# Attention units of a fused attention and feed-forward kernel: another order of ScalarE's, VectorE's and GpSimd's steps

## The chip, the cores and the metric

One core of a Trainium2 chip runs the whole program. The metric is the device time of one execution in microseconds (us). A number with a plain "us" is from one profiled execution; the times of repeated runs are given as their median.

The engines are TensorE (PE; its weight loads PEld), VectorE (DVE), ScalarE (ACT), GpSimd (POOL) and SyncE (SP), which issues most DMAs. Every engine takes its instructions in the order of its own queue and waits, at each, for the semaphores of what that instruction needs.

## The reference, cut to what matters

```python
scores = q @ k.T / sqrt(D)                       # B=2, H=8, S=768, D=64
is_global = pos[None, :] < n_global              # n_global = 8
is_local = (rel >= 0) & (rel < n_local)          # rel = row - column, n_local = 96
dist = where(is_global & ~is_local, n_local, abs(rel))
scores = where(is_global | is_local, scores - slope[h] * dist, -1e9)
a = exp(scores - max); a = a / (a.sum() + 1e-9)
x = (a @ v), heads side by side                  # 1536 tokens x 512
h = x @ w_in;  x = (h * sigmoid(h)) @ w_out      # 512 -> 2048 -> 512
h = x @ w_in2; y = (h * clip(h + 3, 0, 6) / 6) @ w_out2
```

The weights are 64-bit floats in memory; the kernel decodes them on the chip into a high and a low half.

## The kernel before, in words

**Attention units.** The attention is cut into 16 units: a batch, a half of the 768 rows (384 rows, three tiles t of 128) and a pair of heads. Only the keys near a tile and the first 32 are used, so a tile's scores are 128 wide (first tile of a first half) or 256 wide. Unit u takes three steps, n = 3u, 3u+1 and 3u+2, called a, b and c here; the loop over n runs from 0 and calls `attention_loop(n)`, then at most one feed-forward piece, then `turns(n)`, then the weight steps that fall due.

- Step a: `scores` (line 362; TensorE, 12 products into four PSUM banks of the tags S and o), `values(u-2)` (line 411: TensorE's products of the transposed exponentials with the values, `psO`; ScalarE's copy of the high half, line 424; VectorE's low half `xl`, line 425, is put in front of step b), the exponentials of t = 0, the division of the unit before (`normalise`), and `stage_a(u+1, 0)`: three or four transposes of the keys, ScalarE's copy of them (line 350) and VectorE's one or two small copies into the same tile (lines 351, 353).
- Step b: `xl`, the exponentials of t = 1, and `stage_a(u+1, 1)`: transposes of the queries and ScalarE's scaling of them (line 331), without which the next unit's scores can't start; then the loads of unit u+3.
- Step c: the exponentials of t = 2, and `turn(u-1)` (line 396): transposes of the three tiles of exponentials of the unit before, tile by tile, and their copies to SBUF (t = 0 and 2 on VectorE, line 408; t = 1 on ScalarE, line 406).

`exponentials(u, t)` is, for each of two heads, a VectorE pass that adds the bias to the scores and takes the extreme (line 379), then ScalarE's exponential with the sum beside it (line 383). `normalise` is two tiny VectorE steps on the sums (lines 388, 389) and six scalings on GpSimd (line 393). `patterns` (line 274) makes the two distance tiles from the two input words, `biases(p)` (line 309) scales them on GpSimd for a pair of heads, `beyond` (line 297) sets a flag that is read much later.

**PSUM.** The tag `tr` has three banks; into them go, in this order in every unit, the value products, the transposed keys, the transposed queries, and the three tiles of transposed exponentials. The tag `f` has one bank, for feed-forward pieces beside the attention and for the warm-up products.

**Beside the attention.** From n = 17 on, a piece of the first feed-forward layer goes into TensorE's queue at every second step at most (h pieces of 12 products at n = 17, 23, 29, 35, 41, 47; y pieces of 6 at 31, 33, 37, 39, 43, 45, 49, 51). A weight block of 512 columns is decoded in ten steps, started at n = 0, 6, 12, 18, 26, 32, 38 and 44. Counted from the start s, at the end of the step: `upper` s (ScalarE), `lower` s+1 (ScalarE), clamp s+1 (VectorE, line 986), shift s+2 (line 992), sign s+3 (line 998, two inputs), power s+4 (line 1003), scale s+5 and add s+6 (GpSimd, two inputs, lines 126 and 134), high half s+8 (ScalarE, line 145), low half s+9 (GpSimd, line 148). The piece of n = 17 needs the blocks of s = 0 and 6. From n = 54 on only feed-forward work is left.

**What sets the order.** In a `manual_schedule` region the named engines issue in the order of the program text; an engine that is not named is ordered by the scheduler, which may move a step ahead of or behind others. For the attention steps the region names TensorE, ScalarE and GpSimd (line 770), not VectorE. The prelude (line 734) is a region of all engines.

Of the kernel before, what the change touches and what calls it, by code (L numbers as in the profile page):

```python
# [18 lines left out]
P = 128  # L19
# [9 lines left out]
def attention_ffn_kernel(ctx, tc, q, k, v, n_global, n_local, w_in1, w_out1, w_in2, w_out2, out):  # L29
    nc = tc.nc  # L30
# [3 lines left out]
    NP = H // 2  # L34
    NT = S // P
    HB = 3
# [25 lines left out]
    def bank(tag, name):  # L62
        return psum.tile([P, 512], F32, name=name, tag=tag, bufs=ps_bufs[tag])
# [11 lines left out]
    def load_weights():  # L75
        n = loaded[0]
        if n == len(pieces):
            return
        loaded[0] += 1
        i, j = pieces[n]  # L80
        l, c = chunks[i]
        w_in, w_out = (w_in1, w_out1) if l == 0 else (w_in2, w_out2)
        fw = FC * P
        r = wpool.tile([P, DW, 2], I32, name=f"raw{n}", tag="raw", bufs=2)
        if j < 2:
            src = w_in.bitcast(I32)[2 * j * P:2 * (j + 1) * P, 2 * c * fw:2 * (c + 1) * fw].rearrange("(k p) f -> p k f", p=P)
            nc.sync.dma_start(r.rearrange("p (k f) w -> p k (f w)", k=2), src)
        else:
            row = c * fw + (j - 2) * P
            nc.sync.dma_start(r.rearrange("p e w -> p (e w)"), w_out.bitcast(I32)[row:row + P, :])  # L90
        raws[n] = r
# [122 lines left out]
    units = [(b, half, p) for b in range(B) for half in range(2) for p in range(NP)]  # L214
# [45 lines left out]
    t1 = apool.tile([P, HB, 2, W], F32, name="pat1", tag="z", bufs=ZB)[:, 0]  # L260
# [48 lines left out]
    def biases(p):  # L309

        nbs[p] = [cpool.tile([P, 2, w], F32, name=f"{n}{p}", tag=f"{n}{p}") for n, w in (("nbB", P), ("nbA", W))]
        for nb, dist in zip(nbs[p], (distB, distA)):
            for h in range(2):
                nc.gpsimd.tensor_scalar(out=nb[:, h, :], in0=dist, scalar1=slopes[2 * p + h], scalar2=1.0, op0=ALU.mult, op1=ALU.mult)
# [40 lines left out]
    zt, mnt, smt, ptt, scored = {}, {}, {}, {}, {}  # L355

    def width(u, t):
        return P if units[u][1] == 0 and t == 0 else W

    def scores(u):  # L360

        kt, qt = tr[u]
        two, one = ([bank(tag, f"psS{u}_{tag}{h}") for h in range(2)] for tag in "So")
        place = {(h, t): one[h][:, :W] if t == 2 else two[h][:, t * W:(t + 1) * W] for h in range(2) for t in range(HB)}
        for t in range(HB):
            for h in range(2):
                hs = slice(h * D, (h + 1) * D)
                o = P if width(u, t) == P else t * SP
                nc.tensor.matmul(place[h, t], qt[hs, t * P:(t + 1) * P], kt[hs, o:o + W], start=True, stop=True)  # L369
        scored[u] = place  # L370
        zt[u] = apool.tile([P, HB, 2, W], F32, name=f"z{u}", tag="z", bufs=ZB)
        mnt[u] = apool.tile([P, HB, 2], F32, name=f"mn{u}", tag="mn")
        smt[u] = apool.tile([P, HB, 2], F32, name=f"sm{u}", tag="sm")

    def exponentials(u, t):
        p, w = units[u][2], width(u, t)
        nb, z, mn, sm = nbs[p][w == W], zt[u], mnt[u], smt[u]
        for h in range(2):
            nc.vector.tensor_tensor_reduce(  # L379
                out=z[:, t, h, :w], in0=scored[u][h, t][:, :w], in1=nb[:, h, :], scale=1.0, scalar=3e38,  # L380
                op0=ALU.add, op1=ALU.min, accum_out=mn[:, t, h:h + 1])
        for h in range(2):
            nc.scalar.activation(out=z[:, t, h, :w], in_=z[:, t, h, :w], func=AF.Exp, bias=mn[:, t, h:h + 1], scale=-1.0,  # L383
                                 accum_out=sm[:, t, h:h + 1])

    def normalise(u):
        z, sm = zt[u], smt[u].rearrange("p t h -> p (t h)")
        nc.vector.tensor_scalar(out=sm, in0=sm, scalar1=1e-9, scalar2=None, op0=ALU.add)
        nc.vector.reciprocal(sm, sm)  # L389
        for t in range(HB):  # L390
            w = width(u, t)
            for h in range(2):
                nc.gpsimd.tensor_scalar(out=z[:, t, h, :w], in0=z[:, t, h, :w], scalar1=smt[u][:, t, h:h + 1], scalar2=1.0,  # L393
                                        op0=ALU.mult, op1=ALU.mult)
# [16 lines left out]
    def values(u):  # L411
# [12 lines left out]
        nc.scalar.copy(hi, ps[:, :TB])  # L424
        return lambda: nc.vector.tensor_tensor(out=lo, in0=ps[:, :TB], in1=hi.bitcast(F32), op=ALU.subtract)

    NS = HB * len(units)
    queue, late, rests, now = {}, {}, {}, [0]

# [3 lines left out]
    def attention_loop(n):  # L433
        u, t = divmod(n, HB)
        for f in queue.pop(n, []):
            f()
        if t == 0 and u < len(units):
            scores(u)
        if t == 0 and 0 <= u - 2 < len(units):
            at(n + 1, values(u - 2))  # L440
            if u < len(units):
                loads_v(u)
        if u < len(units):
            exponentials(u, t)
            if t == HB - 1 and u + 1 < NP:
                biases(u + 1)
        if n == 0:
            beyond()
        if t == 0 and 0 <= u - 1 < len(units):
            normalise(u - 1)  # L450
        for f in rests.pop(n, []):
            f()
        if t < 2 and u + 1 < len(units):
            stage_a(u + 1, t)
            if t and u + 3 < len(units):
                loads(u + 3)
# [241 lines left out]
    for l, c in chunks:  # L698
        first_piece[l, c] = len(stream)
        if fast(l, c):  # L700
            p = [(product, l, c, i) for i in (1, 6, 5, 7, 2, 4, 3)]
# [4 lines left out]
            h, y = H(l, c, 2), Y(l, c, 0)  # L706
# [3 lines left out]
        if (l, c) == (1, 0):  # L710

            h = H(l, c, 0) + H(l, c, 1) + H(l, c, 2)
# [21 lines left out]
    with tc.manual_schedule(engines=None):  # L734
        nc.vector.memset(three, 3.0)
        warm = fpool.tile([P, 512], F32, name="warm", tag="a")
        nc.vector.memset(warm, 0.0)
        for _ in range(3):
            nc.tensor.matmul(bank("f", "psW"), warm[:, :P], warm, start=True, stop=True)  # L739
        for i, ap in enumerate((n_global, n_local)):  # L740
            nc.sync.dma_start(nwords[:, i, :], ap.bitcast(I32).partition_broadcast(P))
        loads(0)
        make_identity(nc, ident)
        positions()
        loads(1)
        load_weights()
        loads_v(0)
        load_weights()
        loads(2)
        loads_v(1)  # L750
        load_weights()
        stage_a(0, 0)
        stage_a(0, 1)
        patterns()
        biases(0)
    todo = {when(i): f for i, f in enumerate(stream)}

    def loop(n):
# [8 lines left out]

    E = mybir.EngineType
    end = NS + LAG + 2
    with tc.manual_schedule(engines={E.PE, E.Activation, E.Pool}):  # L770
        for n in range(end):
            if n == NS + LAG:
                ready[0] = 1
            loop(n)
# [261 lines left out]
```

## Time and profile before

| what | value |
|---|---|
| median of 3 runs | 636.79 us (635.80 to 637.16) |
| the profiled execution's own time | 634.86 us |
| its span | 632.8 us |
| TensorE, busy | 606.6 us, 96% of the span |
| VectorE, busy | 464.5 us, 73% |
| ScalarE, busy | 412.9 us, 65% |
| GpSimd, busy | 160.4 us, 25% |
| mean granted clock of TensorE | 0.992 |

The span runs from the first to the last instruction of the profiled execution; some 2 us of the execution's time lie outside it. In the rows below a record has its start, its length, the engine, the line of the kernel, what it writes and reads, and in brackets how long its engine had been idle before it and what ended the wait. A granted clock (PEclk) of 1.00 is the upper of TensorE's two levels, 0.50 the lower. [...]

### The profile page before, as it was taken

To read this page: it belongs to the slowest core of one execution; us is meant where nothing else is said; L and a number is where in the kernel's file an instruction comes from. 1 tells how busy PE (TensorE), PEld (TensorE's weight loads), DVE (VectorE), ACT (ScalarE), POOL (GpSimd) and SP (SyncE) were. 2 spreads that over 40 slices of the span, in tenths; PEclk is the share of its full clock that TensorE was granted. 3 is DMA by queue.
4 is the path that set the end of the run, shared out by engine and by line. 5 is a ranking of instruction groups with operands and counts; after the bars stand their busy time and mean duration, and the time that the engine had idled before them with its cause. 6 is when DMAs were issued, how large, how long until landed. Compare 5 with 4: busy or idle time off the path is not lost.

```text
span 632.8 us, 9365 instructions
## 1 busy us (share of the span) xinstructions
PE 606.6 (96%) x3124; PEld 496.4 (78%) x3124; DVE 464.5 (73%) x1012; ACT 412.9 (65%) x863; POOL 160.4 (25%) x233
## 2 busy tenths in 40 slices
PE   6877999999999999999999999999999999999996
PEld 3656778898888788888888877887788888888885
DVE  5776777734588786767674779987979696969453
ACT  4785878755566676666666676765766666666760
POOL 2764867770111111111111110011111111111100
PEclk9998999999999999999999999999999999999998
DMA  7665556367767858686867791196577768776544
GB/s 173 154 157 124 128 142 147 87 195 141 157 129 158 186 135 183 151 186 151 186 152 154 161 207 67 67 266 151 136 174 163 176 162 177 160 183 151 100 109 162
DMA packets 81622, 97.29 MB, mean 154 GB/s; under 512 B 55456, under 2 KB 55456, under 8 KB 81312
## 3 DMA queue, kind: packets, MB, share of 16 engines
q0 software_dynamic: 12576, 45.09, 38.1%
q1 hardware_dynamic: 68992, 51.53, 27.2%
q8 instruction: 27, 0.44, 0.3%
q14 instruction: 27, 0.22, 0.1%
HBM read 46.27 MB, written 3.15 MB: 78 GB/s over the span
## 4 chain that ended last, share of the span: by engine, by line
PE 58%; issue 23%; POOL 6%; DVE 5%; ACT 5%; DMA 2%; POOLq 0%; DVEq 0%; SPq 0%; ACTq 0%
PE psY L655 25%; PE psH L482 15%; POOL y L684 4%; PE psP_b L563 3%; PE psO L421 3%; PE psT L403 2%; PE psP_c L563 2%; PE psP_a L563 2%; PE psS_S L369 2%; ACT z L383 2%; DMA y<-st 1%; POOL z L393 1%; PE psW L739 1%; PE psS_o L369 1%; DVE z L379 1%
## 5 line engine op out<-in xcount | busy, mean ns | idle before, releaser
L684 POOL DMA_DIRECT2D y<-st x78 | 66.9, 857 | 364.3 <-ACT st L680 359.1
L680 ACT COPY st<-psY 128x512 f32<-128x512 f32 x156 | 91.5, 587 | 52.0 <-PE psY L655 47.9
L482 PE MATMUL psH<-xh,wih 128*128 128x512 f32 (+1 forms) x216 | 83.3, 386 | 2.1 <-DVE g L513 1.5
L482 PE MATMUL psH<-xh,wil 128*128 128x512 f32 (+1 forms) x216 | 82.7, 383 | 2.3 <-POOL wil L148 2.3
L482 PE MATMUL psH<-xl,wih 128*128 128x512 f32 (+1 forms) x216 | 82.7, 383 | 0.0
L655 PE MATMUL psY<-gh,woh 128*128 128x512 f32 (+1 forms) x160 | 61.4, 384 | 0.0
L655 PE MATMUL psY<-gh,wol 128*128 128x512 f32 (+1 forms) x160 | 60.6, 379 | 0.0
L655 PE MATMUL psY<-gl,woh 128*128 128x512 f32 (+1 forms) x160 | 60.5, 378 | 0.0
L655 PE MATMUL psY<-woh,gl 128*128 128x512 f32 x144 | 56.1, 390 | 0.1
L655 PE MATMUL psY<-woh,gh 128*128 128x512 f32 x144 | 56.1, 390 | 0.1
L655 PE MATMUL psY<-wol,gh 128*128 128x512 f32 x144 | 56.0, 389 | 0.0
L393 POOL TENSOR_SCALAR z<-z,sm 128x256 f32<-128x256 f32 (+1 forms) x96 | 45.9, 501 | 26.8 <-DVE sm L389 20.3
L383 ACT ACTIVATE z<-z,mn 128x256 f32<-128x256 f32 (+1 forms) x96 | 46.4, 489 | 3.8 <-DVE mn L379 3.7
L482 PEld LDWEIGHTS psH<-xh,wih 128*128 128x128 f32 x216 | 40.6, 188 | 10.6 <-DVE g L513 1.9
L482 PEld LDWEIGHTS psH<-xh,wil 128*128 128x128 f32 x216 | 40.7, 188 | 9.8 <-POOL wil L148 2.7
L103 ACT ACTIVATE da<-raw 128x512 f32<-128x512 f32 x64 | 43.0, 672 | 6.7 <-DMA raw<-in_moe_w_in_dram 5.3
L482 PEld LDWEIGHTS psH<-xl,wih 128*128 128x128 f32 x216 | 40.7, 188 | 7.5 <-DVE xl L592 0.4
L998 DVE SCALAR_TENSOR_TENSOR da<-raw,da 128x512 int32<-128x512 int32 x64 | 44.2, 690 | 1.1
L986 DVE TENSOR_SCALAR da<-da 128x512 f32<-128x512 f32 x64 | 29.5, 461 | 15.9 <-ACT da L103 15.6
L580 DVE TENSOR_TENSOR u<-psP_c,u 128x512 f32<-128x512 f32 x22 | 15.1, 686 | 34.6 <-ACT u L574 34.6
L504 ACT ACTIVATE a<-psH 128x512 f32<-128x512 f32 (+1 forms) x24 | 14.2, 590 | 40.2 <-PE psH L482 40.2
L523 DVE SCALAR_TENSOR_TENSOR gl<-a,gh 128x512 fp32r<-128x512 f32 (+1 forms) x34 | 23.1, 681 | 22.4 <-ACT gh L517 22.1
(187 smaller groups left out, 1496.9 us busy)
## 6 DMA issues: line engine op xcount, KB each, us to landing
y<-st POOLq DMA_DIRECT2D x78, 512.0 KB, 5.0
raw<-in_moe_w_in_dram SPq DMA_DIRECT2D x32, 512.0 KB, 4.0
raw<-in_moe_w_out_dram SPq DMA_DIRECT2D x32, 512.0 KB, 3.6
rk<-in_k_dram SPq DMA_DIRECT2D x32, 96.0 KB, 3.4
rq<-in_q_dram SPq DMA_DIRECT2D x32, 96.0 KB, 2.5
rv<-in_v_dram SPq DMA_DIRECT2D x32, 96.0 KB, 2.4
out_dram<-y SPq DMA_DIRECT2D x12, 256.0 KB, 2.6
xf<-xh SPq DMA_DIRECT2D x2, 1024.0 KB, 5.2
```

The lines of the kernel that those rows point to most:

```text
L103: nc.scalar.activation(out=t["a"], in_=raws[n][:, :, 1].bitcast(F32), func=AF.Abs)
L369: nc.tensor.matmul(place[h, t], qt[hs, t * P:(t + 1) * P], kt[hs, o:o + W], start=True, stop=True)
L383: nc.scalar.activation(out=z[:, t, h, :w], in_=z[:, t, h, :w], func=AF.Exp, bias=mn[:, t, h:h + 1], scale=-1.0, accum_out=sm[:, t, h:h + 1])
L393: nc.gpsimd.tensor_scalar(out=z[:, t, h, :w], in0=z[:, t, h, :w], scalar1=smt[u][:, t, h:h + 1], scalar2=1.0, op0=ALU.mult, op1=ALU.mult)
L482: nc.tensor.matmul(ps, a[:, kt, js], x[:, kt, n0:n1], start=n == 0, stop=n == 3 * KT - 1)
L523: nc.vector.scalar_tensor_tensor(out=gl[:, j, :], in0=t["a"], scalar=2.0, in1=gh[:, j, :].bitcast(F32), op0=ALU.mult, op1=ALU.subtract)
L563: nc.tensor.matmul(ps, a[:, 2 * k + q, f * P:(f + 1) * P], x, start=p in (1, 5) and n == 0, stop=n == 5, skip_group_check=True)
L655: nc.tensor.matmul(ps[:, :rhs.shape[1]], lhs, rhs, start=n == 0, stop=n == 3 * FC - 1)
L680: nc.scalar.copy(st[:, m % 2, :], part)
L684: late.setdefault(n, []).append(lambda: nc.gpsimd.dma_start(y, st, accum_op=ALU.add))
L986: nc.vector.tensor_scalar(out=a, in0=a, scalar1=as_float(897 << 20), scalar2=as_float((1151 << 20) - 1), op0=ALU.max, op1=ALU.min)
L998: nc.vector.scalar_tensor_tensor(out=ai, in0=w1, scalar=-0x40000000, in1=ai, op0=ALU.bitwise_and, op1=ALU.bitwise_or)
```

## The change

- VectorE is named in the region of the attention steps too: it issues in program order.
- In step a ScalarE's two exponentials of t = 0 stand ahead of its copy of the values.
- `normalise` takes a range of tiles: tiles 0 and 1 are divided in step c of their own unit, right behind the passes of t = 2, and tile 2 in step a of the next.
- `biases(u+1)` moves from step c to step a; `patterns` and `biases(0)` move ahead of `stage_a(0, ...)` in the prelude; `beyond` moves from n = 0 to n = 30.
- Two more warm-up products go into TensorE's queue at n = 2; the three of the prelude stay.

```diff
--- before.py
+++ after.py
@@ -383,11 +383,11 @@
             nc.scalar.activation(out=z[:, t, h, :w], in_=z[:, t, h, :w], func=AF.Exp, bias=mn[:, t, h:h + 1], scale=-1.0,
                                  accum_out=sm[:, t, h:h + 1])
 
-    def normalise(u):
-        z, sm = zt[u], smt[u].rearrange("p t h -> p (t h)")
+    def normalise(u, t0, t1):
+        z, sm = zt[u], smt[u][:, t0:t1].rearrange("p t h -> p (t h)")
         nc.vector.tensor_scalar(out=sm, in0=sm, scalar1=1e-9, scalar2=None, op0=ALU.add)
         nc.vector.reciprocal(sm, sm)
-        for t in range(HB):
+        for t in range(t0, t1):
             w = width(u, t)
             for h in range(2):
                 nc.gpsimd.tensor_scalar(out=z[:, t, h, :w], in0=z[:, t, h, :w], scalar1=smt[u][:, t, h:h + 1], scalar2=1.0,
@@ -424,6 +424,11 @@
         nc.scalar.copy(hi, ps[:, :TB])
         return lambda: nc.vector.tensor_tensor(out=lo, in0=ps[:, :TB], in1=hi.bitcast(F32), op=ALU.subtract)
 
+    def warm_up(n):
+
+        for _ in range(n):
+            nc.tensor.matmul(bank("f", "psW"), warm[:, :P], warm, start=True, stop=True)
+
     NS = HB * len(units)
     queue, late, rests, now = {}, {}, {}, [0]
 
@@ -434,22 +439,26 @@
         u, t = divmod(n, HB)
         for f in queue.pop(n, []):
             f()
-        if t == 0 and u < len(units):
-            scores(u)
+        if u < len(units):
+            if t == 0:
+                scores(u)
+                if u + 1 < NP:
+                    biases(u + 1)
+            exponentials(u, t)
+            if t == 2:
+                normalise(u, 0, 2)
+        if t == 0 and 0 <= u - 1 < len(units):
+            normalise(u - 1, 2, 3)
         if t == 0 and 0 <= u - 2 < len(units):
             at(n + 1, values(u - 2))
             if u < len(units):
                 loads_v(u)
-        if u < len(units):
-            exponentials(u, t)
-            if t == HB - 1 and u + 1 < NP:
-                biases(u + 1)
-        if n == 0:
+        if n == 30:
             beyond()
-        if t == 0 and 0 <= u - 1 < len(units):
-            normalise(u - 1)
         for f in rests.pop(n, []):
             f()
+        if n == 2:
+            warm_up(2)
         if t < 2 and u + 1 < len(units):
             stage_a(u + 1, t)
             if t and u + 3 < len(units):
@@ -735,8 +744,7 @@
         nc.vector.memset(three, 3.0)
         warm = fpool.tile([P, 512], F32, name="warm", tag="a")
         nc.vector.memset(warm, 0.0)
-        for _ in range(3):
-            nc.tensor.matmul(bank("f", "psW"), warm[:, :P], warm, start=True, stop=True)
+        warm_up(3)
         for i, ap in enumerate((n_global, n_local)):
             nc.sync.dma_start(nwords[:, i, :], ap.bitcast(I32).partition_broadcast(P))
         loads(0)
@@ -749,10 +757,10 @@
         loads(2)
         loads_v(1)
         load_weights()
+        patterns()
+        biases(0)
         stage_a(0, 0)
         stage_a(0, 1)
-        patterns()
-        biases(0)
     todo = {when(i): f for i, f in enumerate(stream)}
 
     def loop(n):
@@ -767,7 +775,7 @@
 
     E = mybir.EngineType
     end = NS + LAG + 2
-    with tc.manual_schedule(engines={E.PE, E.Activation, E.Pool}):
+    with tc.manual_schedule(engines={E.PE, E.Activation, E.Pool, E.DVE}):
         for n in range(end):
             if n == NS + LAG:
                 ready[0] = 1
```

## Rows read from the trace of the kernel before

**Rows 1.** windows of 10 us: busy us and count per engine, PEclk, DMA share, GB/s

```profile
150.00:160.00 10.00, 10.00 (x48) 8.58 (x48) 5.54 (x11) 5.82 (x11) 0.00 (x0) 1.00 0.30 78
```

**Rows 2.** timeline, 0 to 30 us: start us, us, engine, line, names, [idle before]

```profile
1.21 0.42 SPq L741 DMA_DIRECT2D nwords<-in_n_local_dram  x1
...
1.50 5.08 PE L739 MATMUL psW<-warm 128*128 128x512 f32 x6 [1.50 <-DVE warm L737]
...
7.77 0.15 DVE L277 SCALAR_TENSOR_TENSOR small<-nwords 128x2 f32<-128x2 int32 x1
...
11.12 0.40 ACT L383 ACTIVATE z<-z,mn 128x128 f32<-128x128 f32 x1 [3.03 <-DVE mn L379]
...
14.64 1.58 PE L369 MATMUL psS_S<-kt,qt 64*128 64x256 f32 x8 [3.81 <-ACT qt L331]
...
20.42 1.13 PE L369 MATMUL psS_S<-kt,qt 64*128 64x256 f32 x8
```

**Rows 3.** TensorE's timeline, 34 to 53 us: starts of units 4 to 6

```profile
34.55 1.13 PE L369 MATMUL psS_S<-kt,qt 64*128 64x256 f32 x8
...
37.68 0.27 PE L336 MATMUL psA<-ident,kp 128*128 128x128 f32 x1
...
41.22 1.13 PE L369 MATMUL psS_S<-kt,qt 64*128 64x256 f32 x8 [0.40 <-ACT qt L331]
...
49.07 0.50 PE L482 MATMUL psH<-xh,wil 128*128 128x384 f32 x1 [2.34 <-POOL wil L148]
...
52.91 1.13 PE L369 MATMUL psS_S<-kt,qt 64*128 64x256 f32 x8
```

**Rows 4.** the chain that ended last, in order of time: start us, us, what

```profile
111.70 1.31 PE psT L403 x12
...
128.48 1.70 PE psO L421 x24
```

**Rows 5.** ScalarE's timeline in unit 4

```profile
37.41 0.48 ACT L424 CAST xh<-psO 128x384 fp32r<-128x384 f32 x1 [2.22 <-PE psO L421]
...
38.78 0.46 ACT L350 COPY kt<-psA 128x384 f32<-128x384 f32 x1
...
39.71 0.50 ACT L383 ACTIVATE z<-z,mn 128x256 f32<-128x256 f32 x1
...
40.70 0.47 ACT L331 ACTIVATE qt<-psA 128x384 f32<-128x384 f32 x1
```

**Rows 6.** VectorE's timeline in unit 4

```profile
35.83 0.42 DVE L379 CUSTOM_DVE_ANT_0 z<-psS_S,nbA 128x256 f32<-128x256 f32 x1 [0.48 <-PE psS_S L369]
...
38.04 0.55 DVE L425 TENSOR_TENSOR xl<-psO,xh 128x384 fp32r<-128x384 f32 x1
...
39.52 0.21 DVE L351 COPY kt<-psA 128x64 f32<-128x64 f32 x1
...
39.85 1.53 DVE L986 TENSOR_SCALAR da<-da 128x512 f32<-128x512 f32 x1
```

**Rows 7.** GpSimd's timeline in units 4 and 5

```profile
39.82 1.28 POOL L134 TENSOR_TENSOR dc<-dc,da 128x512 f32<-128x512 f32 x1
45.03 2.76 POOL L393 TENSOR_SCALAR z<-z,sm 128x256 f32<-128x256 f32 x6 [3.93 <-PE psA L336]
47.75 1.27 POOL L148 TENSOR_TENSOR wil<-dc,wih 128x512 fp32r<-128x512 f32 x1
```

**Rows 8.** loads of the two words (tile nwords)

```profile
DMA to landing us min/median/max: 2.6/3.0/3.3
```

**Rows 9.** windows of 2 us, columns as in rows 1

```profile
16.00:18.00 2.00, 2.00 (x10) 1.00 (x6) 1.75 (x13) 1.12 (x6) 0.55 (x2) 0.50 0.45 96
```

**Rows 10.** line 998 (the sign step), 0 to 140 us

```profile
L998 DVE SCALAR_TENSOR_TENSOR da<-raw,da x8: 692/693/730, 14.6 to 124.7; 128x512 int32<-128x512 int32 x8
```

**Rows 11.** line 351, 0 to 140 us: VectorE idle before it until (us, times)

```profile
  ACT kt L350: 8.8, 7
```

**Rows 12.** page, part 5: busy us, mean ns | idle before, releaser

```profile
L986 DVE TENSOR_SCALAR da<-da 128x512 f32<-128x512 f32 x64 | 29.5, 461 | 15.9 <-ACT da L103 15.6
```

## The prediction

> **What bounds the kernel now.** I read the windows of 10 us first. From 140 us on TensorE is busy all the time [rows 1]; nothing there is touched by the change, so a microsecond won earlier is a microsecond of the whole. Before that lies the attention stage, where TensorE waits. Its 16 units follow each other by the starts of their score products; the starts of units 1, 2, 5 and 6 are at 14.64, 20.42, 41.22 and 52.91 us [rows 2, 3], and unit 15 ends where the value products behind it start, at 128.48 [rows 4]. So units 2 to 4 take 20.80 us, unit 5 takes 11.69, units 6 to 15 take 75.57.
>
> Then I read ScalarE's timeline of unit 4 [rows 5]: the copy of the values (37.41) comes first, then two exponentials, the copy of the keys (38.78) and a weight step, two exponentials (39.71, 0.99 for both) and the scaling of the queries (40.70, 0.47), whose end at 41.17 lets unit 5 start at 41.22 [rows 3]. ScalarE's order is what ends a unit there. VectorE did all six score passes of the unit from 35.83 on, and the low half of the values (38.04) and the two small key copies (from 39.52 to 39.85) after them [rows 6]: the scheduler had put the passes ahead.
>
> Unit 5 is special. TensorE waits 2.34 us for the low half of the first weights, and that piece of GpSimd (47.75) stands behind six scalings that started only at 45.03 [rows 3, 7].
>
> **What the change does, part by part.** A measurement of this kernel can tell about 0.2%, 1.3 us, from no change.
>
> *Patterns first.* Step 277 starts at 7.77 now, behind the key copies of unit 0; its words, issued at 1.21, take 3.3 us to land [rows 2, 8], so it can start at 4.6, some 3.2 us earlier. Then biases are ready before the first scores. The first score pass can start 1.28 us after its products, as in unit 4 (35.83 against its products at 34.55) [rows 3, 6], at 9.4. From there by ScalarE's order: two narrow exponentials of 0.40 each from 9.75 (11.12 now [rows 2]), key copy from 10.55, on VectorE the small copy behind it and score pass b from 11.2, a weight step on ScalarE meanwhile, two exponentials 1.00 from 11.8, queries 0.47: unit 1 starts at 13.3, 1.35 earlier. Putting `beyond` at step 30 costs its six tiny operations there, in a gap of VectorE between scores and key copies.
>
> *warm_up(2).* The granted clock from 16 to 18 us is 0.50, the lower level, behind a wait of 3.81 us [rows 2, 9]. Three such products took 5.08 us at the start [rows 2], 1.7 each; two take 3.4 at that speed and 1.7 at twice of it. They begin where TensorE's wait before unit 1 begins, at 10.8 (14.64 less 3.81), and end at 12.5 or 14.2. I take 12.5, since the clock is seen low only behind that wait, not ahead of it: hidden until 13.3. The other end costs 1.0.
>
> *Unit 1* in the new order. VectorE's program order inside a unit (steps a, b, c) is: score pass a, end of the last sums, key copies, weight step; low half of values, score pass b, weight step; score pass c, first sums, two copies of transposed tiles, weight step. Unit 1 then takes 6.2: 2.4 until ScalarE's key copy, behind its exponentials; that copy 0.46, the small copy 0.13, a sign step 0.69 [rows 10], the pass until its exponential can start 0.46, two exponentials 1.00, queries 0.52, the last transposes 0.45. Unit 2 starts at 19.5, **0.9 earlier**.
>
> *The chain of a normal unit.* Exponentials of step a now run while TensorE makes the value products, which takes 1.0 us out of ScalarE's chain. But VectorE in program order makes a new one. Start from unit 4's own times. The key transposes end at 37.95 [rows 3]; key copy on ScalarE 37.98 to 38.44; VectorE's small key copies wait for it (seven waits on just that) [rows 11] and take 0.33 with their handoffs, to 38.80; they stand ahead of the low half of the values, 0.55 recorded and 0.47 to the next, to 39.27; score pass b until its exponential can start 0.46; two exponentials 0.99; queries 0.47 and 0.05 to TensorE: 41.24, the time of before. Then comes a further term: the three banks of `tr` hold value products, keys and queries, so the third transposed tile gets one only when the queries are scaled, or later. Its four transposes, a third of 1.31 [rows 4], 0.45, now stand behind the queries and ahead of the next scores. Unit 4 takes 7.2 where it took 6.67.
>
> Units differ from this by what VectorE does after the small key copies, ahead of the low half: nothing in 2, 4, 6, 8; the sign step, 0.69 [rows 10], in 3, 5, 7; clamp in 9 and power in 10, 12, 14, 0.4 to 0.46 by the mean of clamps [rows 12]. With value products of full width (units 6 to 9, 14, 15) the key copy comes 0.2 later; without the second small copy (2, 7 to 10) 0.2 less. Adding: units 2 to 4: 7.0, 8.2 (0.26 in it because the clamp of unit 2 meets GpSimd, below), 7.2, sum 22.4, **1.6 longer**. Units 6 to 10, 12, 14: 7.4, 7.9, 7.2, 7.7, 7.4, 7.6, 7.8. Units 11, 13, 15 hold two FFN pieces and are bound by TensorE before and after: 8.5, 8.65, 8.2, of which 0.2 to 0.4 is won since ScalarE's copy of the first piece is no longer behind exponentials. Sum 78.35, **2.8 longer**.
>
> *Sums in two groups.* GpSimd gets four of six scalings a step earlier, and the low half of the first weights (step 15) stands behind two scalings instead of six. Sums of the last tile come at 2.1 us of unit 5, scalings 0.92, low half 1.27: ready at 4.5, and TensorE asks for it 5 us into the unit. The stall goes; late next is VectorE's chain with its sign step. Unit 5 takes 7.9, **3.8 shorter**. If its cover were gone, the wait would be one low half, 1.27 [rows 7]. What is queued behind the new wait: VectorE stands at the first sums until the second exponentials are done, and both copies of transposed tiles stand behind it; they are wanted by value products only in the next unit, so this costs nothing as long as no transposed tile needs a bank from them.
>
> *Contention.* A clamp that met GpSimd's two-input add of 1.28 us took 1.53 instead of the mean 0.46 [rows 6, 7, 12]. The sign step is never longer than 0.73 in the attention stage [rows 10], and no row shows it beside such an add, so I take nothing; its upper bound is 1.28 each. [...]
>
> Sum: 0.9 - 1.6 + 3.8 - 2.8 = **0.3 us won**. The profiled span of 632.8 becomes 632.5; with 2.1 outside it 634.6 against 634.86. The median of the runs shown stands 1.9 above the profiled one, so 636.5 against 636.79.
>
> **Rivals.**
>
> *The key copies do not hold VectorE.* If the wait for ScalarE's copy [rows 11] came only from where the scheduler had put them, they would start with the end of the key transposes, 0.5 earlier in each of eleven units bound by the chain: 5.5 us, 631.0. For it: nine of sixteen copies showed no such wait. Against: these came late anyway, and both write into one tile.
>
> *Sign steps held by GpSimd.* In units 3, 5 and 7 the low half of a weight (1.27) follows the last two scalings on GpSimd, some 3.1 to 4.4 us into the unit, and the sign starts at 4.25. If it waits for such an instruction and GpSimd runs late by some 0.5, each unit pays 0.7; with the power and clamp steps of 9 to 14 paying 0.1 each some 2.7 in all: 639.2, slower. It decides from the point where GpSimd is 0.5 late; for it the clamp's 1.53, against it the 0.69 of the sign.
>
> *Banks from the copies.* If the second transposed tile, too, gets its bank from the copy of the first, which now stands behind the first sums, a unit pays 1.0 more: eleven units, 647. The scheduler had handed out a bank in this manner while key copies came late; now they come early, so I hold it unlikely.
>
> **How the numbers follow.** Forecast 0.37, its own range 634 to 638.5 (warm_up's 1.0, and 0.15 to either side in each of eleven chains). Key copies free, or some other link of the chain shorter than I have it: 0.30. Sign steps held: 0.20. Banks: 0.08. The rest, 0.05, a stall of unit 5 that stays in part. The range takes in the first three, 630.5 to 640.5. Faster by over 0.2%: 0.30 and 0.11 of the forecast's low end, 0.41. Slower: 0.20, 0.08, 0.03 and little of the rest, 0.31. Same 0.28.
>
> **What would show it.** In the profile after: VectorE's pattern steps near 4.6; unit 1's scores near 13.3 at full clock; exponentials ahead of the value copy, and TensorE's wait for the weights' low half gone, with units 5 and 6 some 8 us apart instead of 11.69; the last four transposes of a unit right behind the scaling of the queries; chain-bound units of 7.2 and, with a sign, 7.9. It is wrong if those units come out near 6.5 (then the time is near 631), or above 8, or if sign steps are longer than 0.73.

## The result, and the profile after

| | before | after |
|---|---|---|
| median, runs on the same chip | 636.29 us (634.59 to 637.16, 4 runs) | 644.47 us (642.71 to 645.57, 4 runs) |
| the profiled execution, its span | 634.86 us, 632.8 us | 645.02 us, 642.7 us |
| mean granted clock of TensorE | 0.992 | 0.989 |

The ratio of after to before is 1.0129, 95% interval 1.0096 to 1.0162: 8 us slower, where 0.3 us faster was forecast. It lies outside the range, on its slow side.

**Where the time was lost.** The last value products of the attention stage, at 128.48 us before [rows 4], start at 136.98: 8.5 us of the 9.9 by which the span grew. The rest of the program takes as long as it did, to within a microsecond and a half. The first rows to read are the page's head after, and then the waits of TensorE from 0 to 140 us (engine, line, waited for: us in total, times, longest).

```profile
span 642.7 us, 9408 instructions
...
PE 612.1 (95%) x3128; PEld 498.2 (78%) x3128; DVE 469.5 (73%) x1044; ACT 415.9 (65%) x863; POOL 157.9 (25%) x233
```

```profile
PE psT L403 <- ACT qt L331: 12.8, 12, 1.8
```

The same view of before:

```profile
PE psS_S L369 <- ACT qt L331: 4.8, 4, 3.8
...
PE psH L482 <- POOL wil L148: 2.3, 1, 2.3
```

And the start of the last value products after, in TensorE's timeline:

```profile
136.98 0.49 PE L421 MATMUL psO<-pt,vp 128*64 128x128 f32 x4
```

Two things stand in these rows. TensorE is *busy* for 5.5 us more than before (612.1 against 606.6), though two warm-up products of some 1.1 us each are all it was given in addition, and its first three account for only 1.2 more (6.28 us against 5.08): part of the loss is slower work, not waiting. And the waits have changed their kind. The one wait for the first weights' low half is gone; in its place the last transposes of a unit (line 403) wait for the scaled queries (line 331), twelve times.

**The chain of a unit** is the forecast one, link by link. Here is unit 4 after, ScalarE's, VectorE's and TensorE's records together; it answers to [rows 5, 6]:

```profile
37.39 1.14 PE L369 MATMUL psS_S<-kt,qt 64*128 64x256 f32 x8
...
40.82 0.48 ACT L350 COPY kt<-psA 128x384 f32<-128x384 f32 x1
...
41.33 0.22 DVE L351 COPY kt<-psA 128x64 f32<-128x64 f32 x1 [1.22 <-ACT kt L350]
...
41.67 0.55 DVE L425 TENSOR_TENSOR xl<-psO,xh 128x384 fp32r<-128x384 f32 x1
...
42.13 0.41 DVE L379 CUSTOM_DVE_ANT_0 z<-psS_S,nbA 128x256 f32<-128x256 f32 x1
...
42.59 0.51 ACT L383 ACTIVATE z<-z,mn 128x256 f32<-128x256 f32 x1 [0.73 <-DVE mn L379]
...
43.59 0.47 ACT L331 ACTIVATE qt<-psA 128x384 f32<-128x384 f32 x1
...
44.20 0.63 PE L403 MATMUL psT<-ident,z 128*128 128x128 f32 x4 [1.21 <-ACT qt L331]
44.76 1.76 PE L369 MATMUL psS_S<-kt,qt 64*128 64x256 f32 x8
```

VectorE stands idle 1.22 us at the small key copy until ScalarE's key copy is done; the low half, the score pass, the exponentials, the queries and the last transposes follow one another without a gap. Unit 4 takes 7.37 us, from 37.39 to 44.76 (7.2 forecast; 6.67 before). The small copy waits so in every unit; the row of before counted seven such waits [rows 11], this is line 351 after, from 0 to 140 us:

```profile
  ACT kt L350: 22.3, 16
```

**What the forecast did not have** is the clock. TensorE's timeline after, and windows of 2 us (columns as in [rows 1]; the clock is the third number from the end):

```profile
20.00 0.63 PE L403 MATMUL psT<-ident,z 128*128 128x128 f32 x4 [1.82 <-ACT qt L331]
20.55 1.45 PE L369 MATMUL psS_S<-kt,qt 64*128 64x256 f32 x8
...
29.41 1.14 PE L369 MATMUL psS_S<-kt,qt 64*128 64x256 f32 x8
...
109.31 0.63 PE L403 MATMUL psT<-ident,z 128*128 128x128 f32 x4 [1.21 <-ACT qt L331]
109.87 2.00 PE L369 MATMUL psS_S<-kt,qt 64*128 64x256 f32 x8
```

```profile
22.00:24.00 2.00, 2.00 (x17) 1.35 (x16) 0.76 (x6) 0.88 (x4) 2.00 (x5) 0.50 1.14 267
...
46.00:48.00 2.00, 2.00 (x16) 1.27 (x14) 1.07 (x7) 1.47 (x5) 0.52 (x2) 0.50 0.54 122
...
110.00:112.00 2.00, 2.00 (x10) 1.68 (x12) 0.67 (x1) 1.55 (x5) 2.00 (x4) 0.50 0.39 83
```

Three times up to 600 us the granted clock goes from 1.00 to 0.50 (windows of 1 us show these two values, and others only at the change), each time just behind a wait of the last transposes for the queries (1.82, 1.21 and 1.21 us); the eight score products that take 1.13 or 1.14 us elsewhere take 1.45, 1.76 and 2.00 there. The units in which it happens, 2, 5 and 13, took 8.86, 9.54 and 10.24 us against 7.0, 7.9 and 8.65 forecast. No other unit is off by as much as 0.8.

**The sign step**, for whose meeting with GpSimd the forecast took nothing, was held four times. GpSimd and VectorE in unit 12, and all eight sign steps (ns, shortest, median, longest):

```profile
102.04 1.27 POOL L148 TENSOR_TENSOR wil<-dc,wih 128x512 fp32r<-128x512 f32 x1
102.24 1.62 DVE L1006 SCALAR_TENSOR_TENSOR da<-raw,da 128x512 int32<-128x512 int32 x1
...
103.78 0.41 DVE L379 CUSTOM_DVE_ANT_0 z<-psS_S,nbA 128x256 f32<-128x256 f32 x1
```

```profile
L1006 DVE SCALAR_TENSOR_TENSOR da<-raw,da x8: 681/848/1622, 17.3 to 137.7; 128x512 int32<-128x512 int32 x8
```

GpSimd's instruction with two inputs ends at 103.31, the sign 0.55 later at 103.86; the three others (66.26, 120.83 and 137.70) also end 0.55 behind GpSimd's. A sign takes 0.68 or 0.69 alone (17.32, 33.70 and 50.67), so the author reads these four as held until GpSimd's instruction ends; the records show the ends, not what holds them. In units 12 and 14 the sign stands ahead of the first score pass, and the whole unit waits with it; the last one delays a gate step, for which TensorE waits 0.58 at 139.88. Beside GpSimd's scalings, which read one tensor in SBUF, no such delay shows: the sign at 86.25 took 0.68 within a run of four scalings from 85.16 to 87.28, and the four signs of before that fell into such runs took at most 0.73 [rows 10].

**The parts that went as forecast.** The start (VectorE's first pattern step, the three warm-up products, unit 1's scores) and the first weights' low half with the piece that needs it:

```profile
1.50 6.28 PE L430 MATMUL psW<-warm 128*128 128x512 f32 x6 [1.50 <-DVE warm L746]
...
4.66 0.16 DVE L277 SCALAR_TENSOR_TENSOR small<-nwords 128x2 f32<-128x2 int32 x1 [2.30 <-DMA nwords<-in_n_local_dram]
...
14.35 1.13 PE L369 MATMUL psS_S<-kt,qt 64*128 64x256 f32 x8 [0.27 <-ACT qt L331]
```

```profile
48.77 1.27 POOL L148 TENSOR_TENSOR wil<-dc,wih 128x512 fp32r<-128x512 f32 x1
...
49.87 0.43 PE L491 MATMUL psH<-xh,wih 128*128 128x384 f32 x1
```

The piece at 49.87 runs without the wait of 2.34 us that it had [rows 3]. Patterns start at 4.66 as worked out. Unit 1 starts 5.01 us behind unit 0 (5.16 forecast), but at 14.35 and not at 13.3, because unit 0 itself started at 9.34 where the execution of before had 8.14: the three warm-up products, which are the same in both kernels, took 6.28 us in place of 5.08 [rows 2].

### The profile page after: what moved, and what is told of

The parts are those of the page before. It is cut to its first block, busy times and chain, and to the rows that moved or that the text cites. A ratio compares the mean times of both kernels' runs of the same rounds, so it can differ in the third digit from the quotient of the medians.

```text
span 642.7 us, 9408 instructions
## 1 busy us (share of the span) xinstructions
PE 612.1 (95%) x3128; PEld 498.2 (78%) x3128; DVE 469.5 (73%) x1044; ACT 415.9 (65%) x863; POOL 157.9 (25%) x233
## 4 chain that ended last, share of the span: by engine, by line
PE 35%; issue 25%; POOL 5%; DVE 2%; DMA 2%; ACT 1%; POOLq 0%; ACTq 0%; SPq 0%; DVEq 0%
PE psY L664 19%; PE psH L491 9%; POOL y L693 5%; PE psP_b L572 3%; PE psP_c L572 2%; PE psP_a L572 2%; DMA y<-st 1%; DMA raw<-in_moe_w_in_dram 1%; ACT st L689 0%; DVE g L522 0%; DVE da L1006 0%; DVE wol L148 0%; DVE u L589 0%; ACT da L103 0%; DVE dc L134 0%
## 5 line engine op out<-in xcount | busy, mean ns | idle before, releaser
L393 POOL TENSOR_SCALAR z<-z,sm 128x256 f32<-128x256 f32 (+1 forms) x96 | 44.1, 475 | 49.1 <-DVE sm L389 35.7
L1006 DVE SCALAR_TENSOR_TENSOR da<-raw,da 128x512 int32<-128x512 int32 x64 | 46.9, 733 | 1.0
L403 PE MATMUL psT<-ident,z 128*128 128x128 f32 x176 | 25.7, 277 | 17.8 <-ACT qt L331 12.8
```

What stands on the lines that cost most here:

```text
L403: nc.tensor.transpose(ps[:, h, c, :], z[:, t, h, c * P:(c + 1) * P], ident)
L1006: nc.vector.scalar_tensor_tensor(out=ai, in0=w1, scalar=-0x40000000, in1=ai, op0=ALU.bitwise_and, op1=ALU.bitwise_or)
```

## The experiments

Ratios are to the kernel before, run beside each on the same chip; 0.01 of the ratio is 6.4 us. Line numbers are those of each run's own kernel, a few off from the kernel after where lines were added or cut.

### Is it VectorE's program order? One part out, one part alone

First the change without VectorE in the region (called the free order from here on), and the kernel before with VectorE in it and nothing else.

```diff
-    with tc.manual_schedule(engines={E.PE, E.Activation, E.Pool, E.DVE}):
+    with tc.manual_schedule(engines={E.PE, E.Activation, E.Pool}):
```

> All of the change but one thing: the scheduler orders VectorE again. Theory (VectorE's program order makes the chain small key copies, low half of the values, score pass b, exponentials b, queries, last transposes): the chain goes, the exponentials ahead of the value copy keep their 1 us a unit, so well below before, 628 to 634 us, and the last transposes of a unit start before the queries are scaled. Rival (the loss comes from the other parts: sums in two groups, biases, warm-up): it stays near 644.

Measured: 625.67 us (625.21 to 626.32), ratio 0.9838 [0.9822, 0.9855]. Even below the range of the theory: everything else in the change wins 10 us, and the order of VectorE alone turns that into a loss of 8. Unit 4 of this run:

```profile
32.99 1.13 PE L369 MATMUL psS_S<-kt,qt 64*128 64x256 f32 x8
...
36.05 0.42 DVE L379 CUSTOM_DVE_ANT_0 z<-psS_o,nbA 128x256 f32<-128x256 f32 x1
...
36.40 0.55 DVE L425 TENSOR_TENSOR xl<-psO,xh 128x384 fp32r<-128x384 f32 x1
...
36.93 0.23 DVE L351 COPY kt<-psA 128x64 f32<-128x64 f32 x1
...
38.88 1.13 PE L369 MATMUL psS_S<-kt,qt 64*128 64x256 f32 x8
```

All six passes, the last at 36.05, are over before the key copy is there; the low half fills the time, and the small copy finds its input ready (it has no wait). The unit takes 5.89 us, from 32.99 to 38.88, where it took 7.37 after. The mean granted clock is 0.999: none of the stage's windows of 10 us is below 1.00.

```diff
-    with tc.manual_schedule(engines={E.PE, E.Activation, E.Pool}):
+    with tc.manual_schedule(engines={E.PE, E.Activation, E.Pool, E.DVE}):
```

(in the kernel before)

> The kernel before with VectorE in program order and nothing else of the change. Theory: the same chain, and behind it the key copy that still waits for two exponentials, so slower than the changed kernel in the units bound by the chain and with the stall of unit 5 still there: 648 to 660 us. Rival (other parts): near the kernel before, 636.

Measured: 661.26 us (660.76 to 663.02), ratio 1.0407 [1.0388, 1.0426], just above the range. The order costs 26 us on the old text and 18.5 on the new (1.0129 less 0.9838); the rival, that it costs nothing by itself, falls. TensorE's waits, and a window of 10 us, show the same two losses as after, the wait for the queries and a clock that falls:

```profile
PE psT L403 <- ACT qt L331: 10.8, 9, 2.0
```

```profile
40.00:50.00 10.00, 7.60 (x47) 5.48 (x47) 4.05 (x20) 5.19 (x17) 4.92 (x8) 0.66 0.45 117
```

### Is it the chain through key copies, low half, pass and queries?

Two ways to cut the chain and keep the program order: the queries ahead of the exponentials that wait for VectorE, or VectorE's passes ahead of the key copies that wait for ScalarE.

```diff
@@ attention_loop(n), ahead of exponentials(u, t)
+            if t == 1 and u + 1 < len(units):
+                stage_a(u + 1, 1)
@@ and where stage_a stood
-            stage_a(u + 1, t)
+            if t == 0:
+                stage_a(u + 1, 0)
```

> The changed kernel with the scaling of the queries (and their transposes) ahead of the exponentials of step b. Theory: the third bank comes free before the chain's end and the next scores wait no longer for the exponentials of step b, so TensorE's wait of 1.2 us before the last four transposes goes in every unit and a unit takes some 6.3 instead of 7.5: 632 to 637 us. Rival: 644.

Measured: 632.9 us, ratio 0.9947 [0.993, 0.9964], within the theory's range and 11.6 us better than after. The queries no longer wait for VectorE, nor the transposes for the queries: in unit 4 ten of them run in one go ahead of the next scores, and of the 12.8 us of such waits one wait of 0.7 is left.

```profile
38.71 0.49 ACT L331 ACTIVATE qt<-psA 128x384 f32<-128x384 f32 x1
...
38.85 1.55 PE L403 MATMUL psT<-ident,z 128*128 128x128 f32 x10 [0.79 <-ACT da L103]
```

```profile
PE psT L403 <- ACT qt L331: 0.7, 1, 0.7
```

```diff
@@ exponentials(u, t): all six passes in step a
-        for h in range(2):
-            nc.vector.tensor_tensor_reduce(
...
+        for i in range(HB) if t == 0 else ():
+            w, nb = width(u, i), nbs[p][width(u, i) == W]
+            for h in range(2):
+                nc.vector.tensor_tensor_reduce(
...
```

> The changed kernel with VectorE's six score passes of a unit all in step a, ahead of the small key copies. Theory: the exponentials of step b start right behind the key copy, 1.2 us earlier (1.9 where a sign step stands in between), the last transposes still wait for the queries: units some 1 us shorter, 631 to 637 us. Rival: 644.

Measured: 634.02 us, ratio 0.9967 [0.9953, 0.9981], within range too. Either cut takes more away than the change had lost (11.6 and 10.3 us), so the chain is shown from both ends. In neither run does the clock fall in the attention stage (1.00 in every window of 10 us up to 150), so these sums hold the price of the three falls too, which is measured below. What is late next in this run is new:

```profile
PE psY L667 <- DVE g L525: 4.6, 4, 1.3
```

The gate products of a feed-forward piece (VectorE) now stand behind six passes. That asks whether both cuts together reach the time of the free order.

```diff
@@ the two cuts in one kernel
+        for i in range(HB) if t == 0 else ():
...
+            if t == 1 and u + 1 < len(units):
+                stage_a(u + 1, 1)
```

> The changed kernel, VectorE in program order, with both: queries ahead of the exponentials of step b, and the six score passes together in step a. Theory: program order itself costs nothing once the order has no chain in it, so it reaches the kernel with VectorE left to the scheduler: 624 to 628 us. Rival (an engine that must keep program order loses in any order): 631 to 634, no better than either move alone.

Measured: 632.69 us, ratio 0.9951 [0.9934, 0.9968]. The rival was right: with the chain cut twice nothing more is won than with one cut. TensorE's waits (here line 670 is the second layer's product, line 528 the gate):

```profile
PE psY L670 <- DVE g L528: 5.3, 4, 1.6
PE psH L497 <- POOL wil L148: 2.2, 1, 2.2
```

The two rows, 7.5 us, are about as long as the distance to the free order (7.0 by medians). That they make it up is not shown by this run. Was it that place in the text? The next run writes the gate steps ahead of the passes:

```diff
@@ attention_loop(n), on top of both cuts
         for f in queue.pop(n, []):
             f()
+        for f in rests.pop(n, []):
+            f()
...
-        for f in rests.pop(n, []):
-            f()
```

> The kernel of e5_both (program order, queries ahead of the exponentials of step b, all six passes in step a), with the gate steps of a feed-forward piece (VectorE's clamp and products, GpSimd's and ScalarE's part of them) written ahead of the passes of their step, not behind them. Theory (a wait of VectorE in program order moves to whatever stands last: in e5_both the y pieces waited 5.3 us for gate products behind passes and sums): the four waits go or shrink below 0.5 us each, 3 to 5 us of 632.69 are won, 627.5 to 630. The passes come about 0.6 us later in units 6, 7, 9 and so on, and the exponentials with them, which may cost up to 0.5 in each of five units. Rival (in program order each place costs as much as the other, or the stall for the weights' low half holds the time): 631.5 to 634.

Measured: 630.31 us, ratio 0.9913 [0.989, 0.9935], at the upper edge of the theory's range, 0.3 above it, and 2.4 us better than without by the ratios, whose intervals just touch each other. Three of the four waits went, the fourth stayed, and small key copies began to be waited for:

```profile
PE psT L406 <- DVE kt L353: 2.5, 3, 1.0
...
PE psY L670 <- DVE g L528: 1.0, 1, 1.0
```

So the theory holds for the waits that were named, and the rival for a part of the gain: each place written earlier makes another later. The best text in program order that was tried is still 4.6 us behind the order of the scheduler.

### What is the clock's share?

The kernel after with one warm-up product (nothing reads its result) ahead of the last transposes of two units, then of six, so that TensorE works while it would wait for the queries.

```diff
@@ turn(u), t == 2
+            if t == 2 and u in (0, 3):
+                warm_up(1)
```

> The changed kernel (VectorE in program order) with one warm-up product more ahead of the last transposes of units 1 and 4, where TensorE waits 1.2 to 1.8 us for the queries. Theory (the chain's waits let the granted clock fall at 21 and at 45 us, and what unit 2 and unit 5 take over the worked-out chain is this): the clock stays at 1.00 there, units 2 and 5 take some 7.3 and 8.0 instead of 8.9 and 9.5: 641 to 642.5 us. Rival (units 2 and 5 are long for another reason): 644.5 or more.

Measured: 647.54 us, ratio 1.0177 [1.015, 1.0205]: a miss, 3 us slower and not 3 faster. The two units behaved as worked out (7.24 and 8.18 us, down from 8.86 and 9.54), but the clock fell in others, units 3 and 9, and again in 13 (0.50 from 110 to 112 us). Windows of 2 us:

```profile
28.00:30.00 2.00, 2.00 (x12) 1.45 (x10) 1.16 (x4) 1.53 (x5) 1.76 (x4) 0.50 0.60 135
...
76.00:78.00 2.00, 2.00 (x10) 1.50 (x10) 0.89 (x2) 2.00 (x6) 1.42 (x4) 0.50 0.60 133
```

The stage ended where it ended after; another 2 us came behind it, in a further fall between 200 and 250 us (0.97 in the mean of these 50, 1.00 after) that has no part in the attention. The two falls that were taken from units 2 and 5 turned up in two other units that wait; so six units at once:

```diff
-            if t == 2 and u in (0, 3):
+            if t == 2 and u in (0, 1, 2, 3, 5, 7):
```

> The changed kernel with a warm-up product ahead of the last transposes of units 1, 2, 3, 4, 6 and 8. Theory (the clock falls wherever the chain's waits add up, and a fall costs 1.6 us of the stage): no fall before 70 us, units 2, 3 and 5 at 7.3, 7.9 and 8.1, the stage two falls or 3 us shorter: 641 to 643 us against 644.5 to 647. Rival (falls only move to other units, three in all): 644 to 648.

Measured: 639.89 us, ratio 1.0065 [1.0048, 1.0082], 1.1 below the theory's range and far from the rival's. The windows in which the clock had fallen after are at full clock:

```profile
22.00:24.00 2.00, 1.90 (x22) 1.28 (x17) 0.75 (x5) 1.84 (x7) 2.00 (x6) 1.00 1.18 283
...
46.00:48.00 2.00, 2.00 (x15) 1.89 (x13) 1.31 (x4) 0.56 (x2) 1.42 (x2) 1.00 0.47 107
...
110.00:112.00 2.00, 1.76 (x12) 1.49 (x11) 1.56 (x7) 1.44 (x3) 0.45 (x1) 1.00 0.58 132
```

Unit 2 as an example:

```profile
19.96 1.14 PE L369 MATMUL psS_S<-kt,qt 64*128 64x256 f32 x8
...
27.20 1.13 PE L369 MATMUL psS_S<-kt,qt 64*128 64x256 f32 x8
```

Units 2, 5 and 13 take 7.24, 8.18 and 8.62 us here against 8.86, 9.54 and 10.24: 4.6 us less together; the ratios differ by 4.1 us. So the clock had cost between 4.1 and 4.6. With it held the kernel is still 4 us slower than before: the chain and the held signs, less what the other parts win.

### What are the other parts worth?

Each of these is the kernel with VectorE left to the scheduler (625.67 us, 0.9838) with one more part undone.

ScalarE's copy of the values ahead of the first exponentials again:

```diff
@@ attention_loop(n), ahead of exponentials(u, t)
+            if t == 0 and 0 <= u - 2 < len(units):
+                at(n + 1, values(u - 2))
...
```

> VectorE ordered by the scheduler, the rest of the change kept, but ScalarE's copy of the values ahead of the exponentials of step a again. Theory (that order is worth up to 1 us in each unit that ScalarE's chain ends, and nothing where TensorE is full): 629 to 634 us against 625.7. Rival (the sums in two groups and the start give all of the gain): 626.

Measured: 629.23 us, ratio 0.9895 [0.9872, 0.9917]; 3.6 us lost, in the lower part of the range. It is seen in ScalarE's waits at that copy from 0 to 140 us, in this run and then in the free order with the exponentials ahead of it:

```profile
ACT xh L424 <- PE psO L421: 23.7, 16, 2.8
```

```profile
ACT xh L424 <- PE psO L421: 4.2, 7, 1.5
```

The sums in one group again:

```diff
-            if t == 2:
-                normalise(u, 0, 2)
...
-            normalise(u - 1, 2, 3)
+            normalise(u - 1, 0, 3)
```

> VectorE ordered by the scheduler, the rest of the change kept, but the sums of a unit divided in one group, in step a of the next unit. Theory (two groups take away the stall of unit 5): the wait for the low half of the first weights is back, 2.3 us and some 1.5 us of low clock behind it: 629 to 631 us. Rival (the stall goes by the earlier exponentials alone): 626.

Measured: 628.49 us, ratio 0.9878 [0.986, 0.9895]; 2.5 us lost, 0.5 below the theory's range. The stall of before is back in its old size, and unit 5 takes 10.21 us:

```profile
PE psH L489 <- POOL wil L148: 2.4, 1, 2.4
```

The low clock that was expected behind it does not show. Behind the stall of before the clock had fallen (0.50 from 50 to 52 us), and the twelve transposes there took 2.65 us; in this run they take 1.47:

```profile
50.33 2.65 PE L403 MATMUL psT<-ident,z 128*128 128x128 f32 x12
```

```profile
47.21 1.47 PE L403 MATMUL psT<-ident,z 128*128 128x128 f32 x12
```

The old start (patterns and first biases behind the transposes, no further warm-up products, the flag at n = 0):

```diff
+        stage_a(0, 0)
+        stage_a(0, 1)
         patterns()
         biases(0)
-        stage_a(0, 0)
-        stage_a(0, 1)
...
-        if n == 2:
-            warm_up(2)
```

> VectorE ordered by the scheduler, the rest of the change kept, but the start as before: patterns behind the transposes of unit 0, no two further warm-up products, the flag at step 0. Theory (the new start is worth 1.3 us up to unit 1 less what the later first scores take back, and holds the clock in units 1 and 2): 626.5 to 628 us, and a lower clock after unit 1's scores. Rival (the first scores come 1.2 us later because of the patterns): 625 and first scores near 8.2 us.

Measured: 628.62 us, ratio 0.9877 [0.9861, 0.9894]; 0.6 above the theory's range and 2.5 us lost by the ratios, though only 1.4 by the profiled spans (625.1 against 623.7), in which unit 0 starts at 8.45 here and at 9.40 in the free order. Behind unit 1's first scores the products are slow as before, where the clock was 0.50 from 16 to 18 us: the next four score products take 1.07 us in both (0.60 in unit 2), so the low clock that was expected shows in them. The three parts sum to 8.6 of the 10.3 us that the change without the order wins; the earlier biases were not run by themselves.

Last, the free order with the queries ahead of the exponentials of step b, the cut that had won 11.6 us in program order:

```diff
-    with tc.manual_schedule(engines={E.PE, E.Activation, E.Pool, E.DVE}):
+    with tc.manual_schedule(engines={E.PE, E.Activation, E.Pool}):
...
+            if t == 1 and u + 1 < len(units):
+                stage_a(u + 1, 1)
```

> VectorE left to the scheduler, the rest of the change kept, and the queries ahead of the exponentials of step b. Theory: with the passes early the units after the eighth are nearly full on TensorE, and what is left of its waits before (some 3 us from 10 to 60 us) shrinks a little: 623 to 626 us. Rival (the exponentials become late and the copies of transposed tiles wait): 627 to 630.

Measured: 628.34 us, ratio 0.9867 [0.9827, 0.9906]: the rival. Nothing is won, and the interval leaves open whether something is lost. The profiled execution is 4.5 us longer in its span than that of the free order, but its unit 15 starts at 110.33 against 110.30: the difference lies behind the units. The mean granted clock of this execution is 0.995, against 0.999. What repairs the queue in program order is of no use where that queue does not hold the unit.

The change without VectorE in the region, at 625.67 us, is faster than the kernel before and than the changed one, and the best of all that ran.

## Why the prediction was wrong

**Right: the mechanism and the parts.** Patterns at 4.6 (4.66 measured), the warm-up products hidden, the stall of unit 5 gone, the small key copies as the wait of VectorE, the third transposed tile behind the queries: each shows in the profile after where the text said it would, and cutting the chain at either end (632.9 and 634.02 us) shows that it sets the time. Two of the text's sums are off by little: the terms of unit 1 add to 6.11 us, not 6.2, and those of unit 4 to 7.14, not 7.2; neither made the miss. The units that met neither the clock nor a held sign come out close to their sums: 7.37, 7.59, 7.45 and 7.57 us for units 4, 6, 8 and 10, against 7.2, 7.4, 7.2 and 7.4.

The rival that key copies do not hold VectorE is refuted: they held it in all sixteen units. The rival that a bank comes from the copies did not happen.

**Wrong, first: the term for the clock was missing.** The step that failed is the sum of *the chain of a normal unit* and the units listed behind it, made at full clock throughout. The text had seen the clock fall behind a wait of 3.81 us (0.50 from 16 to 18 us), and asked of the warm-up products only whether they were hidden. It did not ask what its own chain would do: the last transposes wait 1.2 to 1.8 us for the queries nine times in sixteen units, and the clock fell behind three of these waits (0.50 from 22, from 46 and from 110 us). The price, from the run with six warm-up products, is 4.6 us by the units (4.1 by the ratios). Before, the clock had fallen twice, behind the 3.81 us and in unit 5 behind its 2.34 us (0.50 from 50 to 52). The change takes both falls away, as the run in free order shows (1.00 in every window of 10 us up to 150), and VectorE's order brings three new ones.

**Second: nothing was taken for the held signs.** The row with the clamp of 1.53 us beside GpSimd's add [rows 6, 7] was read as a case of the clamp alone. Units 7, 12 and 14, in which a held sign stands on the chain, came out 0.5, 0.75 and 0.55 us above their sums, and the last held sign cost a wait of 0.58: 2.4 us at most, since small differences are in it. The rival *sign steps held* priced that at 2.7 and was right in kind, but it had put them into units 3, 5 and 7, of which only 7 had one; in 12 and 14 it is the sign of the step before that runs over into the next unit's first pass, a place that the forecast did not look at. No run moved the signs away, so this price is read from the records alone.

**Third: the start.** Unit 2 was forecast at 19.5 us and started 1.05 later, and the late unit 0 accounts for it. Whether the change has a part in this stays open: unit 0 started at 8.14, 8.45 and 8.62 us in the three profiles with the old start, and between 8.51 and 9.62 in the eleven with the patterns first, one profile of each kernel. The row that goes with it is the length of the same three warm-up products (5.08 to 5.55 us in the three, 5.04 to 6.34 in the eleven).

The rest of the difference in the span, 10.2 us against the forecast 632.5, is made up of differences between -0.2 and 0.3 us in eleven sums of units (1.4 together), and 0.8 behind the chain, where the stage of feed-forward pieces begins (1.4 with the wait of 0.58). Added: 4.6, 1.8 in the three units with signs, 1.05, 1.4 and 1.4 give 10.2.

**The choice that mattered** is none of these sizes, though. The forecast set the gains (0.9 and 3.8) against the chain (1.6 and 2.8) as if they were one bundle. The runs show that they are two: parts worth 10 us without the order, and an order that costs 18.5, its clock falls included. The gain of the exponentials, 3.6 us when measured alone, was worked out as taken back by VectorE's new chain; the record of unit 4 agrees, but no run tests it in program order.

What stays open: which of the waits lets the clock fall in one unit and not in the next that waits as long. Its length alone does not settle it: behind the stall of 2.34 us for the first weights the clock fell before, and behind the same stall of 2.25 and 2.35 us in the runs with both cuts and with the gate steps first it did not (1.00 in every window of 10 us up to 140), nor do the products behind the 2.38 us in the run with one group show it (1.47 us for twelve transposes, 2.65 before). And the y-piece waits that follow the two cuts were removed only in part, so how far a program order could be brought is not known; 630.31 us is the best tried.

## What to carry to other kernels

Before an engine is put into program order, list for each of its instructions that waits for another engine what stands behind it in the queue and who waits for that; here one small copy held the low half, the score pass, the exponentials and the next unit, and each cure by rewriting moved the wait to the next such place. When a forecast puts a wait into every round of TensorE, forecast the clock as well, with the price of a fall from the profile's own slow stretch (here three of nine waits of 1.2 to 1.8 us had one behind them, and the three cost 4.6 us by the units, an estimate of 1.5 each). And where a change has several parts, price the parts apart: the best version was the change without one of them.

## What the runs showed of the hardware that had not been expected

- TensorE's granted clock fell to 0.50 behind three of nine waits of 1.2 to 1.8 us that come again from unit to unit, with work between them, and not only behind the long wait of 3.81 us [rows 2, 9]; behind single waits of 2.25 and 2.35 us it stayed at 1.00 in two runs, and in a third the twelve transposes behind 2.38 us took 1.47 us, against 2.65 at 0.50. With two of these waits covered the falls came in other units (0.50 from 28 and from 76 us) and again from 110; with six covered the windows of 2 us in which the clock had been 0.50 in either run were at 1.00.
- The four sign steps of VectorE (two inputs) that started while a GpSimd instruction with two inputs ran ended some 0.55 us after it: 1.62, 1.62, 1.39 and 1.01 us in place of 0.69, with 1.07, 1.08, 0.84 and 0.46 of GpSimd's 1.27 us left. Beside GpSimd's scalings with one tensor input the sign took 0.68 to 0.73.
- The same three first products took from 5.04 to 6.34 us from one profiled run to another (6.34 in three, among them the one with the gate steps first, where unit 0 starts at 9.62), and the first scores mostly move with them.
